# Small vectors loaded as single runs, z's turn in two PSUM places, and a new written order for the opening of a gated scan with two MLPs

## The chip, the cores and the metric

The kernel runs on one core of a Trainium2 chip. The metric is device time in microseconds. The engines are TensorE (PE, with its weight loads as PEld), VectorE (DVE), ScalarE (ACT), GpSimd (POOL) and SyncE (SP, which here only issues DMAs).

## The reference, cut to what matters

```python
# x, f_logit: (1, 6080, 256); lower_bound: (256,)
sig = 1.0 / (1.0 + np.exp(-f_logit))
f = lower_bound + (1.0 - lower_bound) * sig
for t in range(S):
    h = f[:, t] * h + (1.0 - f[:, t]) * x[:, t]
    y[:, t] = h
# first MLP: w_in (256, 2048), w_out (2048, 256), a (4), b (2)
h = y @ w_in
P = a[0] + a[1] * h + a[2] * h**2 + a[3] * h**3
Q = 1.0 + np.abs(b[0]) * np.abs(h) + np.abs(b[1]) * h**2
z = (P / (Q + 1e-6)) @ w_out
# second MLP: its own w_in (256, 2048), w_out (2048, 256)
out = np.maximum(z @ w_in, 0.0) ** 2 @ w_out
```

`f_logit` is called z in the kernel. All weights arrive as 64-bit floats.

## The kernel before

The 6080 tokens are cut into twelve blocks, the first of 448 tokens and the others of 512. Channels lie on the partitions (256 channels are two halves, `dc` 0 and 1), tokens run along the row. The first MLP's 2048 hidden channels are worked off in eight chunks of 256. For block j and chunk i, `mm1` makes h in PSUM (L398 for the very first, L357 for all others), a chain of steps on ScalarE, VectorE and GpSimd makes the ratio P / Q, and `mm2` (L376) adds its product with `w_out` into `acc`. The second MLP does the same with `hb` (L357), `relu` and `r2` (the square) on ScalarE, and `s2` (L376).

From block 2 on a regular loop does this (`S1_mm1`, `S2_mm1` and the rest). Blocks 0 and 1, the conversion of the weights, and block 0's second MLP are the opening. Its order is a list of some 400 steps in the string `FIRST`, written out by hand; each engine takes its own steps in the order of that list. A step's number is its chunk: `0` to `7` are block 0's, `8` to `9` and `A` to `F` block 1's. The second digit, where there is one, is a half. The steps that the prediction speaks of:

- `low`, `scale`, `bits` and a unit such as `i13b` (first MLP's `w_in`, fourth quarter, second half; `o` is `w_out`, `i2`/`o2` the second MLP's): from the 64-bit words, GpSimd (VectorE for i13b, i10b and o10) takes the low bits (L173), ScalarE scales the high ones (L169), VectorE joins them (`bits`, L184).
- `dhi`, `neg`, `dlo`: split a converted weight into a high and a low part for blocks 1 and later: two DMAs issued by GpSimd (L205, L207), and a step on ScalarE (L206) between them.
- `mul00`, `scan00`, `mul01`, `scan01`: block 0's product and scan for the two channel halves, on VectorE (L274, L324). `gate`, `pg`, `mul`, `scan` and `turn`, `in` are the same for block 1, where `gate` needs another table on ScalarE.
- in the chain of a chunk: `abs` or `absq` and `lin` on ScalarE; `sq` on ScalarE (block 0) or on GpSimd (block 1, L756); `poly` on VectorE, two instructions that read h in PSUM (L485, L486); `q` on TensorE (L790) or VectorE; `rsq`, `usq` on ScalarE; `rt` (L809), `rs` (L815), `g` (L520) on VectorE.
- `x1h`, `x1l` and `xbh`, `xbl`: split the scanned block 1 or 2 into a high and a low part (`xbl` on VectorE, L894).

h has one PSUM buffer `h1` in `ps_h` (block 0's odd chunks, and chunk 9, use `acc2` in `ps_a`), so a chunk's `mm1` can begin when the `poly` of the chunk that last had the buffer is done. The loop's first `mm1` follows that of chunk F in `h1`.

Ahead of the list stand the loads: z and x of block 0 as rows of 1 KB on SyncE's queue, three small vectors on ScalarE's (L628 to L630), then the weights, each load 512 KB. TensorE turns z and x (L246) with matmuls on random work around them (`warm`, L653, the fillers).

Of the kernel before, what the change touches and what calls it, by code (L numbers as in the profile page):

```python
# [8 lines left out]
F32 = mybir.dt.float32  # L9
# [5 lines left out]
ALU = mybir.AluOpType  # L15

P = 128
# [9 lines left out]
def hgru_two_moe_kernel(  # L27
# [39 lines left out]
    lbt = const.tile([P, KD], F32, name="lbt")  # L67
# [167 lines left out]
    def first_turn(nm, pool, tag):  # L235
# [3 lines left out]
        if tag == "hb":  # L239
            os = [pool.tile([P, NMAX], F32, tag=tag, name=nm + "t") for _ in range(KD)]  # L240
        else:
            o = pool.tile([P, KD, NMAX], F32, tag=tag, name=nm + "t")
            os = [o[:, dc, :] for dc in range(KD)]
# [381 lines left out]
    with tc.manual_schedule():  # L625
        row_load("z", zf, 0, "A")
        row_load("x", xf, 0, "x2l")
        nc.scalar.dma_start(out=lbt, in_=lower_bound.rearrange("(p k) -> p k", k=KD))  # L628
        nc.scalar.dma_start(out=pna, in_=moe_a.partition_broadcast(P))
        nc.scalar.dma_start(out=pb, in_=moe_b.partition_broadcast(P))  # L630
# [15 lines left out]
        nc.vector.tensor_scalar(out=al, in0=lbt, scalar1=-0.5, scalar2=0.5, op0=ALU.mult, op1=ALU.add)  # L646
        nc.vector.tensor_scalar(out=be, in0=lbt, scalar1=0.5, scalar2=0.5, op0=ALU.mult, op1=ALU.add)
# [9 lines left out]
        warm(diag[:M, 0, :], diag[:M, 0, :], 9)  # L657
        zt = first_turn("z", ps_a, "acc2")
        raw = pt["x", 0]
        warm(diag[:M, 0, :], diag[:M, 0, :], 4)  # L660
        xt = first_turn("x", ps_b, "hb")
        warm(raw[:M, 0, :P], raw[:M, 0, :], 3)
        first_gate(zt)
        nc.scalar.activation(out=pb, in_=pb, func=ACTF.Abs)
# [175 lines left out]
        def other_step(what, arg):  # L840
# [250 lines left out]
```

## Time and profile before

| | us |
|---|---|
| median of 3 runs | 1092.63 (1092.56 to 1092.89) |
| profiled execution, its own time | 1093.02 |
| its span, first to last instruction | 1091.0 |
| TensorE busy | 1076.8 (99%) |
| VectorE busy | 953.9 (87%) |
| ScalarE busy | 878.9 (81%) |
| GpSimd busy | 319.4 (29%) |

Busy times are of the span; a matmul's end is modelled, so a busy TensorE is not one at its peak. The granted clock of TensorE is 1.00 of full speed in nearly all of the span (mean 0.999).

### The profile page before, as it was taken

What the parts mean: (1) busy time and instruction counts of PE and PEld (TensorE: products, weight loads), DVE (VectorE), ACT (ScalarE), POOL (GpSimd) and SP (SyncE); (2) the same over time, 40 slices, a digit from 0 to 9 for tenths busy, and PEclk for the clock granted to TensorE, in tenths of its full rate; (3) what the DMA queues carried; (4) which work ended last, traced back from release to release, by engine and by line L of the source; (5) the groups of instructions that cost most, each with busy time, mean ns of one, the idle gap of its engine ahead of it and who ended that gap; (6) DMA issues with size and microseconds to landing.
All of it is one profiled execution on the core that took longest, in us unless ns stands there. A gap on an engine that the chain in (4) does not pass through costs nothing.

```text
span 1091.0 us, 12474 instructions
## 1 busy us (share of the span) xinstructions
PE 1076.8 (99%) x4596; PEld 859.5 (79%) x4596; DVE 953.9 (87%) x870; ACT 878.9 (81%) x987; POOL 319.4 (29%) x245
## 2 busy tenths in 40 slices
PE   8999999999999999999999999999999999999998
PEld 5457757888888888888888888888888888888887
DVE  6999999899899989989989989989989998998732
ACT  6998767978878888888798887887888878877763
POOL 4875531322312232222231222131222122222100
PEclk9999999999999999999999999999999999999999
DMA  9969512500300300200200120030030020010010
GB/s 325 361 186 211 107 40 54 109 10 1 58 1 1 59 1 1 38 20 1 39 20 1 18 40 1 1 59 1 1 59 1 1 40 19 1 20 1 1 20 20
DMA packets 106444, 53.04 MB, mean 49 GB/s; under 512 B 91920, under 2 KB 93840, under 8 KB 106384
## 3 DMA queue, kind: packets, MB, share of 16 engines
q1 hardware_dynamic: 99968, 35.21, 13.5%
q0 software_dynamic: 4896, 16.78, 6.6%
q8 instruction: 36, 0.59, 0.2%
q10 hardware_dynamic: 1520, 0.27, 0.1%
q14 instruction: 24, 0.20, 0.1%
HBM read 29.23 MB, written 6.23 MB: 33 GB/s over the span
## 4 chain that ended last, share of the span: by engine, by line
PE 89%; DVE 6%; DMA 3%; issue 1%; SPq 1%; DVEq 0%
PE acc L376 45%; PE hb L357 23%; PE h L357 21%; DMA wi<-in_moe_w_in_dram 3%; DVE g L520 1%; DVE s L815 1%; DVE t L809 1%; DVE s L485 1%; DVE s L486 1%; DVE sg L324 1%; DVE t L782 1%; DMA wo<-in_moe_w_out_dram 1%; SPq L130 0%; SPq L232 0%; DVE t L827 0%
## 5 line engine op out<-in xcount | busy, mean ns | idle before, releaser
L357 PE MATMUL hb<-x2h,wi 128*128 128x512 f32 (+1 forms) x768 | 204.4, 388 | 0.0
L577 POOL TENSOR_TENSOR g2l<-r,g2h 128x1024 fp32r<-128x1024 f32 x78 | 188.5, 2416 | 18.3 <-PE acc L376 16.2
L1007 POOL COPY turn<-t 128x1 f32<-128x1 f32 x78 | 14.3, 184 | 559.0 <-DVE t L493 559.0
L357 PEld LDWEIGHTS hb<-x2h,wi 128*128 128x128 f32 x768 | 144.2, 188 | 29.5 <-issue 0.4
L376 PE MATMUL acc<-g2h,wo 128*128 128x512 f32 x664 | 164.2, 389 | 0.0
L376 PEld LDWEIGHTS acc<-g2h,wo 128*128 128x128 f32 x664 | 124.8, 188 | 25.9
L512 ACT ACTIVATE u<-t 128x1024 f32<-128x1024 f32 x80 | 85.0, 1063 | 70.2 <-DVE t L493 70.1
L469 ACT ACTIVATE u<-h,pb 128x1024 f32<-128x1024 f32 x80 | 89.3, 1116 | 60.6 <-PE h L357 60.6
L493 DVE SCALAR_TENSOR_TENSOR t<-t,pb,u 128x1024 f32<-128x1024 f32 x80 | 101.8, 1272 | 30.0 <-ACT t L470 30.0
L486 DVE SCALAR_TENSOR_TENSOR s<-s,pna,h 128x1024 f32<-128x1024 f32 (+1 forms) x96 | 121.9, 1270 | 3.4
L357 PE MATMUL hb<-x2l,wi 128*128 128x512 f32 (+1 forms) x384 | 117.4, 387 | 0.0
L485 DVE TENSOR_TENSOR s<-s,h 128x1024 f32<-128x1024 f32 (+1 forms) x96 | 115.5, 1203 | 1.2 <-ACT s L762 0.8
L539 DVE SCALAR_TENSOR_TENSOR g1h<-s,pna,u 128x1024 fp32r<-128x1024 f32 x80 | 102.4, 1280 | 13.2 <-ACT u L513 7.5
L357 PE MATMUL h<-x1h,wc 128*128 128x512 f32 x352 | 110.3, 394 | 0.9 <-DVE s L486 0.9
L555 ACT ACTIVATE r<-hb 128x512 f32<-128x512 f32 (+1 forms) x178 | 95.5, 586 | 17.7 <-PE hb L357 17.7
L357 PE MATMUL h<-x1l,wc 128*128 128x512 f32 x352 | 108.6, 389 | 0.0
L357 PE MATMUL h<-x1h,wd 128*128 128x512 f32 x352 | 108.5, 389 | 0.0
L542 DVE SCALAR_TENSOR_TENSOR t<-t,g1h 128x1024 f32<-128x1024 f32 x80 | 98.1, 1226 | 9.1 <-DVE g1h L539 0.5
L545 DVE SCALAR_TENSOR_TENSOR t<-s,pna,t 128x1024 f32<-128x1024 f32 x80 | 102.8, 1285 | 2.8
L548 DVE TENSOR_TENSOR g1l<-t,u 128x1024 fp32r<-128x1024 f32 x80 | 98.0, 1225 | 7.7
L561 ACT ACTIVATE r<-r 128x1024 f32<-128x1024 f32 (+1 forms) x95 | 100.0, 1053 | 2.6
L572 ACT ACTIVATE g2h<-r 128x1024 fp32r<-128x1024 f32 x83 | 88.2, 1062 | 14.6 <-PE acc L376 9.3
(153 smaller groups left out, 1895.5 us busy)
## 6 DMA issues: line engine op xcount, KB each, us to landing
wi<-in_moe_w_in_dram SPq DMA_DIRECT2D x16, 512.0 KB, 11.3
wo<-in_moe_w_out_dram SPq DMA_DIRECT2D x16, 512.0 KB, 10.6
out_dram<-o SPq DMA_DIRECT2D x84, 64.0 KB, 2.0
z<-in_f_logit_dram SPq DMA_DIRECT2D x40, 128.0 KB, 3.3
x<-in_x_dram SPq DMA_DIRECT2D x40, 128.0 KB, 3.2
wi<-wa POOLq DMA_DIRECT2D x8, 512.0 KB, 6.5
wo<-whole POOLq DMA_DIRECT2D x8, 512.0 KB, 4.5
wc<-wa POOLq DMA_DIRECT2D x4, 512.0 KB, 6.7
```

Source lines behind the costliest of these rows:

```text
L357: nc.tensor.matmul(out=o, lhsT=ws[a][:, k, fs], rhs=xs[b][:, k, :n], start=(q == 0 and k == 0), stop=(q == len(terms) - 1 and k == KD - 1),)
L376: nc.tensor.matmul(out=acc[dc][:, ts], lhsT=ws[a][:, c, dc::KD] if spread else ws[a][:, c, dc * P:(dc + 1) * P], rhs=gs[b][:, c, ts], star ...
L485: nc.vector.tensor_tensor(out=s, in0=s, in1=h, op=ALU.mult)
L486: nc.vector.scalar_tensor_tensor(out=s, in0=s, scalar=pna[:, 1:2], in1=h, op0=ALU.add, op1=ALU.mult)
L493: nc.vector.scalar_tensor_tensor(out=t, in0=t, scalar=pb[:, 1:2], in1=u, op0=ALU.mult, op1=ALU.add)
L539: nc.vector.scalar_tensor_tensor(out=fh, in0=s, scalar=pna[:, 0:1], in1=u, op0=ALU.add, op1=ALU.mult)
L542: nc.vector.scalar_tensor_tensor(out=t, in0=t, scalar=QC, in1=f32(fh), op0=ALU.add, op1=ALU.mult)
L545: nc.vector.scalar_tensor_tensor(out=t, in0=s, scalar=pna[:, 0:1], in1=t, op0=ALU.add, op1=ALU.subtract)
L548: nc.vector.tensor_tensor(out=fl, in0=t, in1=u, op=ALU.mult)
L555: nc.scalar.activation(out=r[:, c, :], in_=h2.pop((*b, c))[:, :m], func=ACTF.Relu)
L561: nc.scalar.activation(out=r, in_=r, func=ACTF.Square)
L577: eng.tensor_tensor(out=gl, in0=r, in1=f32(gh), op=ALU.subtract)
```

## The change

Three things are changed. The small vectors (`lower_bound`, `moe_a`, `moe_b`) are loaded as one run each into a single partition of a tile `few`, and matmuls with one row of `few` put them on all partitions, in a corner of the PSUM tile `idle`; ScalarE and VectorE read them there. Nine fillers stay ahead of z's turn, the four between z's and x's turn go, and the three behind become four. z's two halves are turned into two PSUM tiles, `acc2` and `acc1`, instead of the two halves of one. And the string `FIRST` holds the same 404 steps in another order.

```diff
-            o = pool.tile([P, KD, NMAX], F32, tag=tag, name=nm + "t")
-            os = [o[:, dc, :] for dc in range(KD)]
+            os = [pool.tile([P, KD, NMAX], F32, tag=g, name=nm + "t")[:, 0, :] for g in (tag, "acc1")]
...
-        nc.scalar.dma_start(out=lbt, in_=lower_bound.rearrange("(p k) -> p k", k=KD))
-        nc.scalar.dma_start(out=pna, in_=moe_a.partition_broadcast(P))
-        nc.scalar.dma_start(out=pb, in_=moe_b.partition_broadcast(P))
+        few = io.tile([P, KD, NMAX], F32, tag="x1l", name="few")
+        nc.scalar.dma_start(out=few[0:1, 0, :D], in_=lower_bound.rearrange("(o f) -> o f", o=1))
+        nc.scalar.dma_start(out=few[0:1, 1, 0:4], in_=moe_a.rearrange("(o f) -> o f", o=1))
+        nc.scalar.dma_start(out=few[0:1, 1, 4:6], in_=moe_b.rearrange("(o f) -> o f", o=1))
+        ones = few[0:1, 1, P:2 * P]
+        nc.vector.memset(ones, 1.0)
...
         warm(diag[:M, 0, :], diag[:M, 0, :], 9)
+        lbt = idle[:, 1, 256:256 + KD]
+        for k in range(KD):
+            nc.tensor.matmul(
+                out=idle[:, 1, 256 + k:257 + k], lhsT=few[0:1, 0, k:D:KD], rhs=few[0:1, 1, P:P + 1], start=True, stop=True
+            )
+        nc.vector.tensor_scalar(out=al, in0=lbt, scalar1=-0.5, scalar2=0.5, op0=ALU.mult, op1=ALU.add)
+        nc.vector.tensor_scalar(out=be, in0=lbt, scalar1=0.5, scalar2=0.5, op0=ALU.mult, op1=ALU.add)
         zt = first_turn("z", ps_a, "acc2")
         raw = pt["x", 0]
-        warm(diag[:M, 0, :], diag[:M, 0, :], 4)
         xt = first_turn("x", ps_b, "hb")
-        warm(raw[:M, 0, :P], raw[:M, 0, :], 3)
+        nc.tensor.matmul(out=idle[:, 1, 256:262], lhsT=ones, rhs=few[0:1, 1, 0:6], start=True, stop=True)
+        warm(raw[:M, 0, :P], raw[:M, 0, :], 4)
         first_gate(zt)
-        nc.scalar.activation(out=pb, in_=pb, func=ACTF.Abs)
+        nc.scalar.activation(out=pb, in_=idle[:, 1, 260:262], func=ACTF.Abs)
+        nc.scalar.activation(out=pna, in_=idle[:, 1, 256:260], func=ACTF.Copy)
...
-            "scale i13b, diag, mul00, scan00, low i13b, scale i10a, scale i10b, bits i13b, mul01, scan01, low "
+            "low i10a, low i13b, scale i10a, mul00, scan00, scale i13b, bits i13b, scale i10b, mm1 0a, mul01, "
```

What the new list does on two engines shows in three places. On VectorE, from block 0's gate (`sg`) to the first `poly` (`s<-s,h`), there stood before (`wa<-wi` alone is `low`, with `wi` and `wa` it is `bits`):

```order
L265 TENSOR_SCALAR sg<-sg,al,be 128x448 x2
L274 SCALAR_TENSOR_TENSOR bx<-sg,xt 128x448
L324 SCALAR_TENSOR_TENSOR x_182<-sg,bx 128x448
L173 TENSOR_SCALAR wa_184<-wi_99 128x512
L184 SCALAR_TENSOR_TENSOR wa_184<-wi_99,wa_184 128x512
L274 SCALAR_TENSOR_TENSOR bx<-sg,xt 128x448
L324 SCALAR_TENSOR_TENSOR x_182<-sg,bx 128x448
L173 TENSOR_SCALAR wa_192<-wi_101 128x512
L184 SCALAR_TENSOR_TENSOR wa_192<-wi_101,wa_192 128x512 x2
L173 TENSOR_SCALAR wb_209<-wo_107 128x1024
L334 COPY carry<-x_182 128x1 x2
L485 TENSOR_TENSOR s<-s,h_200 128x2x448
```

and now:

```order
L263 TENSOR_SCALAR sg<-sg,al,be 128x448 x2
L172 TENSOR_SCALAR wa_183<-wi_100 128x512
L272 SCALAR_TENSOR_TENSOR bx<-sg,xt 128x448
L322 SCALAR_TENSOR_TENSOR x_188<-sg,bx 128x448
L183 SCALAR_TENSOR_TENSOR wa_183<-wi_100,wa_183 128x512
L272 SCALAR_TENSOR_TENSOR bx<-sg,xt 128x448
L322 SCALAR_TENSOR_TENSOR x_188<-sg,bx 128x448
L332 COPY carry<-x_188 128x1 x2
L183 SCALAR_TENSOR_TENSOR wa_181<-wi_102,wa_181 128x512
L172 TENSOR_SCALAR wa_181<-wi_102 128x512
L183 SCALAR_TENSOR_TENSOR wa_181<-wi_102,wa_181 128x512
L172 TENSOR_SCALAR wb_226<-wo_108 128x1024
```

The `low` of i13b has moved ahead of the first product and scan, and the carry copies ahead of the conversions of i10.

On ScalarE, from the gate to the first table load behind it, there stood before (`wi_99` is i13, `wi_101` i10):

```order
L264 ACTIVATE sg<-zt 128x448 x2
L664 ACTIVATE pb<-pb 128x2
L169 ACTIVATE wi_99<-wi_99 128x512
L169 ACTIVATE wi_101<-wi_101 128x512 x2
L855 ACT_TABLE_LOAD
```

and now (`wi_100` is i13, `wi_102` i10):

```order
L262 ACTIVATE sg<-zt 128x448 x2
L670 ACTIVATE pb<-idle 128x2
L671 ACTIVATE pna<-idle 128x4
L168 ACTIVATE wi_102<-wi_102 128x512
L168 ACTIVATE wi_100<-wi_100 128x512
L168 ACTIVATE wi_102<-wi_102 128x512
L862 ACT_TABLE_LOAD
```

One half of i10 is now scaled ahead of i13, and `pna` is copied from PSUM.

On VectorE around `poly F` (here `s<-s,h_1036`, two rows), the last step that reads chunk F's h, there stood before (`x1l<-sg,x1h` are `xbl0` and `xbl1`):

```order
L815 SCALAR_TENSOR_TENSOR s<-s,pna,u 128x1024
L520 SCALAR_TENSOR_TENSOR g<-t,s 128x1024
L782 TENSOR_TENSOR t<-t,u 128x1024
L485 TENSOR_TENSOR s<-s,h_1036 128x1024
L486 SCALAR_TENSOR_TENSOR s<-s,pna,h_1036 128x1024
L894 TENSOR_TENSOR x1l<-sg,x1h 128x512 x2
L809 SCALAR_TENSOR_TENSOR t<-t,u 128x1024
L815 SCALAR_TENSOR_TENSOR s<-s,pna,u 128x1024
```

and now (`poly F` is `s<-s,h_1047`):

```order
L518 SCALAR_TENSOR_TENSOR g<-t,s 128x1024
L901 TENSOR_TENSOR x1l<-sg,x1h 128x512
L822 SCALAR_TENSOR_TENSOR s<-s,pna,u 128x1024
L901 TENSOR_TENSOR x1l<-sg,x1h 128x512
L816 SCALAR_TENSOR_TENSOR t<-t,u 128x1024
L518 SCALAR_TENSOR_TENSOR g<-t,s 128x1024
L789 TENSOR_TENSOR t<-t,u 128x1024
L483 TENSOR_TENSOR s<-s,h_1047 128x1024
L484 SCALAR_TENSOR_TENSOR s<-s,pna,h_1047 128x1024
```

The two low parts of block 2's input have moved from behind `poly F` to ahead of it, between steps of chunks D and E.

## Rows read from the trace of the kernel before

**Rows 1.** The page, busy time of each engine (share of the span).

```profile
PE 1076.8 (99%) x4596; PEld 859.5 (79%) x4596; DVE 953.9 (87%) x870; ACT 878.9 (81%) x987; POOL 319.4 (29%) x245
```

**Rows 2.** Busy time by stretch: stretch, its length, then each engine's busy us.

```profile
core 0: us, PE busy (x) PEld busy (x) DVE busy (x) ACT busy (x) POOL busy (x), PEclk, DMA share, GB/s
8.85:20.00 11.15, 7.79 (x26) 4.04 (x26) 8.87 (x14) 7.78 (x12) 6.32 (x4) 1.00 1.05 386
20.00:60.00 40.00, 37.48 (x106) 18.64 (x105) 39.18 (x44) 39.08 (x54) 32.40 (x15) 1.00 1.06 365
60.00:159.30 99.30, 96.86 (x349) 64.68 (x348) 97.53 (x90) 77.44 (x92) 54.75 (x39) 1.00 0.58 129
...
260.00:1060.00 800.00, 800.00 (x3530) 662.43 (x3529) 709.54 (x632) 653.88 (x717) 199.41 (x158) 1.00 0.10 18
```

**Rows 3.** What TensorE waited for from 0 to 260 us, the largest group.

```profile
PE h L357 <- DVE s L486: 2.9, 3, 1.3
```

**Rows 4.** Order of time on TensorE: start, us, line, idle before it.

```profile
5.35 1.70 PE L246 MATMUL zt<-diag,z 112*128 112x112 f32 x8
...
12.27 3.33 PE L398 MATMUL h<-x,wa 128*128 128x448 f32 x8 [1.68 <-DVE wa L184]
...
159.50 0.70 PE L357 MATMUL h<-x1h,wc 128*128 128x512 f32 x2 [0.88 <-DVE s L486]
```

**Rows 5.** Busy time by stretch, early loads: the last two columns are the DMA's.

```profile
3.00:4.00 1.00, 1.00 (x6) 1.00 (x6) 0.00 (x0) 0.72 (x2) 0.00 (x0) 1.00 0.93 307
4.00:7.00 3.00, 3.00 (x17) 3.00 (x16) 0.24 (x2) 0.00 (x0) 0.00 (x0) 1.00 0.80 218
8.00:9.00 1.00, 1.00 (x11) 1.00 (x10) 0.77 (x3) 0.27 (x3) 0.53 (x1) 1.00 1.04 395
```

**Rows 6.** Order of time on VectorE, the front and the first chain.

```profile
7.67 0.95 DVE L265 TENSOR_SCALAR sg<-sg,al,be 128x448 f32<-128x448 f32 x2 [3.19 <-ACT sg L264]
8.85 0.62 DVE L274 SCALAR_TENSOR_TENSOR bx<-sg,xt 128x448 f32<-128x448 f32 x1 [0.23 <-PE xt L246]
...
10.51 0.81 DVE L173 TENSOR_SCALAR wa<-wi 128x512 int32<-128x512 uint32 x1
11.43 0.69 DVE L184 SCALAR_TENSOR_TENSOR wa<-wi,wa 128x512 int32<-128x512 int32 x1
...
13.70 0.40 DVE L173 TENSOR_SCALAR wa<-wi 128x512 int32<-128x512 uint32 x1
...
17.18 1.11 DVE L173 TENSOR_SCALAR wb<-wo 128x1024 int32<-128x1024 uint32 x1 [1.69 <-DMA wo<-in_moe_w_out_dram]
...
18.69 1.09 DVE L485 TENSOR_TENSOR s<-s,h 128x896 f32<-128x896 f32 x1 [0.28 <-ACT s L762]
...
21.94 1.14 DVE L815 SCALAR_TENSOR_TENSOR s<-s,pna,u 128x896 f32<-128x896 f32 x1
```

**Rows 7.** Order of time on ScalarE: i13b and the first half of i10.

```profile
8.99 0.68 ACT L169 ACTIVATE wi<-wi 128x512 f32<-128x512 f32 x1 [0.71 <-DMA wi<-in_moe_w_in_dram]
...
10.34 0.66 ACT L169 ACTIVATE wi<-wi 128x512 f32<-128x512 f32 x1 [0.67 <-DMA wi<-in_moe_w_in_dram]
```

**Rows 8.** Order of time on VectorE, the end of the opening.

```profile
143.07 1.22 DVE L782 TENSOR_TENSOR t<-t,u 128x1024 f32<-128x1024 f32 x1
...
154.79 2.11 DVE L782 TENSOR_TENSOR t<-t,u 128x1024 f32<-128x1024 f32 x1
...
159.26 1.29 DVE L894 TENSOR_TENSOR x1l<-sg,x1h 128x512 fp32r<-128x512 f32 x2
```

**Rows 9.** Order of time on GpSimd, three of its instructions.

```profile
20.41 3.72 POOL L173 TENSOR_SCALAR wb<-wo 128x1024 int32<-128x1024 uint32 x1
...
65.19 0.92 POOL L207 DMA_DIRECT2D wd<-wa  x1 [2.90 <-ACT wd L206]
...
154.73 3.68 POOL L173 TENSOR_SCALAR whole<-wo 128x1024 int32<-128x1024 uint32 x1
```

**Rows 10.** DMA issues from 0 to 60 us: count, KB each, median us to landing.

```profile
wd<-wa POOLq DMA_DIRECT2D x2, 512.0 KB, 8.4
```

More of the change, by code (lines that the diff above doesn't have):

```diff
@@ L66, in hgru_two_moe_kernel @@
     pb = const.tile([P, 2], F32, name="pb")
-    lbt = const.tile([P, KD], F32, name="lbt")
     al = const.tile([P, KD], F32, name="al")
@@ L645, in hgru_two_moe_kernel @@
         nc.scalar.activation(out=turn, in_=turn, func=ACTF.Tanh)
-        nc.vector.tensor_scalar(out=al, in0=lbt, scalar1=-0.5, scalar2=0.5, op0=ALU.mult, op1=ALU.add)
-        nc.vector.tensor_scalar(out=be, in0=lbt, scalar1=0.5, scalar2=0.5, op0=ALU.mult, op1=ALU.add)
         idle = ps_h.tile([P, 2, NMAX], F32, tag="h1", name="idle")
```

63 rows, old and new, of the table FIRST are left out of this document.

## The prediction

> **What bounds the kernel now.** I read the page's busy times first, then busy time by stretch, then what TensorE waits for, then the order of time on each engine. TensorE is busy 99% of the span and VectorE 87% [rows 1]. From 260 to 1060 us TensorE's 800.00 us are all busy [rows 2]: the steady loop can't give anything, since the change leaves it alone. What can move is the moment at which that loop begins. Its first matmul starts at 159.50, after a wait of 0.88 us for VectorE's L486 [rows 4]: it reuses the PSUM tile of step `mm1 F`, and `poly F`, which ends there, is the last to read it. The loop therefore starts when VectorE has reached `poly F`. Between 20 and 159.3 us VectorE is busy 39.18 of 40.00 and 97.53 of 99.30 us, against TensorE's 37.48 and 96.86 [rows 2], and among TensorE's waits in the opening the largest is for VectorE's `s` [rows 3]. So the opening is limited by VectorE, although TensorE is busier over the whole span.
>
> This makes the account short. Up to `poly F` VectorE does the same steps before and after, with one exception below. The loop's start moves by what changes in four things: when VectorE's stream begins, how long it waits in it, how much its instructions are stretched, and which steps stand ahead of `poly F`.
>
> **Small loads.** The three broadcast loads are 128 rows of 8 or 16 bytes each. While they are in flight the DMA engines move 218 GB/s (4 to 7 us), and afterwards 395 [rows 5]. If 4 to 7 us ran at 390, 3 x 172 = 516 KB more would have moved, or 1.3 us at that rate; the queue of weights behind would land that much earlier. The lower bound is nothing, if the low rate is that of z's and x's 1 KB rows; the nearest row, the 307 GB/s that such rows reached a moment earlier (3 to 4 us, [rows 5]), speaks for a gain, so I take 1.3. The new memset and the copy of `pna` cost VectorE and ScalarE under 0.2 us each in gaps. The three small matmuls have no row. Their bounds are nothing and the price of z's turn, 1.70 us for 8 rows of the trace [rows 4], so 0.2 a row; if the two ahead of z's turn make two rows each, as the fillers do, that is 0 to 0.8, and I take 0.3, since one column is far less than 112.
>
> **Front, step by step.** The nine fillers stay, so z's turn starts at 5.35 + 0.3 = 5.65 and takes 1.70 [rows 4]: its end moves from 7.05 to 7.35. VectorE's two `sg` steps took 0.95 from 7.67 [rows 6] and so ended 1.57 after that. The halves are now apart, so that the first is through by then and one step of about 0.5 is left out of the 1.57: they end at about 7.35 + 1.1 = 8.45. Until then x has landed and been turned, since four fillers are gone between the two. VectorE goes on with `low i13b`, moved here from behind `scan00`: 0.40 us without company (it took 0.81 at 10.51 against 0.40 of its like at 13.70, [rows 6]), to 8.85; then `mul00` and `scan00`, 1.7 us by their starts, to 10.6. ScalarE now scales i10a before i13b. i10a landed at 10.3 and i13b at 9.0 [rows 7]; 1.3 us earlier, ScalarE scales i10a from 9.0 and i13b from 9.7 to 10.3. So `bits i13b` (0.69, [rows 6]) runs from 10.6 to 11.3, and the first real matmul starts at 11.4 instead of 12.27 [rows 4]. The same 0.85 us carries through `scan01`, the first `sq` and `lin` to `poly 0` (before 18.69, [rows 6]), because o10, for which VectorE waited 1.69 us, lands by 15.9 and `low o10` ends by 17.0, ahead of 17.85. **First term: -0.85.** If the small loads change nothing, ScalarE waits for i10a until 10.3, `bits i13b` ends at 12.4, later than before, and the term is +0.2.
>
> **Waits after that.** VectorE waited 0.82 us from 20 to 60 and 1.77 to 159.3 [rows 2]. Adding up the steps in the new order from 14.85 (ScalarE is full: 39.08 of 40, [rows 2]), I find two new ones: `lin 3` now stands behind both gates and a table load and ends at 39.5, where VectorE is there at 38.5; and `usq 5` stands behind `neg i12` and `neg i13`, and VectorE waits 0.65 for it. Some 0.8 of the old waits have no counterpart. Of the new 1.65 about 1.3 fall together with the stretching below: a late VectorE doesn't wait. **Second term: +1.65 - 0.8 - 1.3 = -0.45**, between -0.9 and +0.9.
>
> **Stretched instructions.** Twelve VectorE instructions up to `poly F` take 0.16 to 0.93 us longer than others of their form, 8.3 us in all; the first is `low i13b` (0.81) and the last L782 at 154.79, 2.11 against 1.22 at 143.07 [rows 6, 8]. Each begins within about 1.3 us of a GpSimd instruction's start (here 154.73, [rows 9]), and all but the first take both inputs from SBUF; those that read PSUM, as `poly` does, run at their usual length. GpSimd's list keeps the same eight `sq`, the lows and the gates; only the neighbours change. Which pairs meet can't be read from an order to a fraction of a microsecond. Going through it I find about as many: `bits i13a`, two of the `g`, six of eight `sq`, three lows. **Third term: 0**, the one hit in the first term aside, between -4 and +3.
>
> The Trainium skill's page "SBUF — State Buffer", section "Who interferes with whom", says that a VectorE instruction with two SBUF inputs and a GpSimd instruction that reads SBUF exclude each other, and that the later one waits for the whole of the first. The trace agrees for the short ones and not for the long ones: L815 at 21.94, both inputs in SBUF, begins 1.5 us into a GpSimd `low` of 3.72 us and takes 1.14 [rows 6, 9]. By the page it would have waited until 24.13, 2.2 us; four such meetings in the new order would add some 9 us, to 1101. I go by the row, which gives that no chance.
>
> **Ahead of `poly F`.** The new order puts `xbl0` and `xbl1` before it, which stood behind it and took 1.3 us from 159.26, 1.2 up to the next instruction [rows 8]; they cost the loop's start that much. Before, they were hidden behind the first four of its matmuls. Nothing else changes sides (`q D` and `bits o21` move, but not across it). **Fourth term: +1.2.**
>
> TensorE's own order costs nothing as long as VectorE decides: from 8.85 to 159.3 it has 3.4 + 2.5 + 2.4 us of idle time [rows 2] as cover.
>
> **Sum:** -0.85 - 0.45 + 0 + 1.2 = -0.1 us. The profiled execution took 1093.02 with a span of 1091.0; the runs' median is 1092.63, which is 0.4 below it. The span should stay near 1090.9 and the median near 1092.5.
>
> **Rivals.** *Fewer meetings* (0.25): if the new neighbours halve the stretching, the loop starts about 3.5 to 4 us earlier: 1088.9. For it: six of the twelve lie after 120 us, as the one at 154.79 [rows 8], where a shift by one step would do. Against it: nothing in the order keeps GpSimd's `sq` off them. Its floor is TensorE's own work: 159.50 - 12.27 less 6.8 us idle is 140.4; from 11.4, with some 3 us of waits for ScalarE that stay, the loop begins at 154.8, which is 4.7 us earlier (1087.9).
>
> *More meetings* (0.11): the same at 11 to 12 us of stretching: about 3 us later, 1095.5. It decides from four more hits of 0.9.
>
> *GpSimd late* (0.08, the other side by one mechanism): `mm1 8` now goes before `mm1 9` and needs the low half of i13. Its copy, issued at 65.19 before, when ScalarE had just delivered [rows 9], now queues behind four lows of 3.7 us or more (20.41, [rows 9]), the first of which can't begin before the copies of i10 have landed, by my sum at about 44. That gives an issue at 60.5 and, with the 8.4 us that such copies need [rows 10] a landing at 69; `mm1 8` wants it at 70, and `poly 8` has 2 to 3 us in hand. From four lows of 4.5 instead of 3.7 on it decides, one for one; at 2.5 us the time is 1095.1.
>
> *The small loads don't matter* (0.06): +0.2 instead of -0.85, so 1093.6, still no change by measure.
>
> **How the numbers follow.** About 0.2% (2.2 us) is what a measurement of this kernel can tell from no change. My forecast has 0.50; with the last rival "within 0.2%" has 0.56, faster 0.25, slower 0.11 + 0.08 = 0.19. The range reaches down to the fewer meetings (1089.0) and up to the more (1095.6), and leaves under 2 in 10 outside; the forecast's own range, by its second term and half the third, is 1090.5 to 1094.6.
>
> **What would show it.** Right, if the first matmul after the fillers starts near 11.4, the DMA engines pass 350 GB/s from 4 us on, TensorE's wait before the loop's first matmul is again for `poly F` at about 159, and the stretched instructions again sum to some 8 us. The front is wrong if 12.27 hardly moves; the second term, if VectorE's idle time from 20 to 159 is far from 2.5 us; the third, if stretching is under 5 or over 11 us. The forecast as a whole is wrong if TensorE's opening has no longer VectorE as the engine that it waits for at the end.

## The result, and the profile after

| | before | after |
|---|---|---|
| time, median (lowest to highest) | 1092.83 us (1092.56 to 1093.08, 6 runs) | 1099.44 us (1097.66 to 1104.59, 6 runs) |
| profiled execution, its span | 1093.02, 1091.0 us | 1101.31, 1099.3 us |
| first real matmul / loop's first matmul | 12.27 / 159.50 us [rows 4] | 14.31 / 167.87 us |

The ratio is 1.0066 (95% interval 1.0044 to 1.0088): slower, outside the predicted range. The profiled execution of after is one of its longer ones, 1.9 us above its median; what follows accounts for that execution. The page's busy times and the loop hardly differ from [rows 1, 2]:

```profile
PE 1080.3 (98%) x4596; PEld 861.5 (78%) x4596; DVE 957.3 (87%) x871; ACT 878.9 (80%) x988; POOL 321.6 (29%) x245
```

Busy time by stretch, after (columns as in [rows 2]); the last row is the loop, where TensorE is busy throughout, as before.

```profile
20.00:60.00 40.00, 36.88 (x104) 18.35 (x103) 38.78 (x41) 37.82 (x50) 34.27 (x16) 1.00 0.98 334
95.00:110.00 15.00, 12.97 (x40) 8.40 (x41) 12.03 (x10) 12.08 (x14) 8.76 (x8) 0.89 0.70 167
260.00:1060.00 800.00, 800.00 (x3531) 662.44 (x3530) 713.37 (x636) 654.84 (x719) 201.88 (x160) 1.00 0.10 18
```

So the loss lies ahead of the loop: the span grew by 8.3 us, the loop's start by 8.37. To split it, I take one stretch from the first real matmul to the loop's first, before and then after:

```profile
12.27:159.50 147.23, 140.39 (x469) 86.13 (x469) 142.51 (x142) 122.58 (x153) 91.35 (x55) 1.00 0.73 206
```

```profile
14.31:167.87 153.56, 142.45 (x469) 87.15 (x469) 146.68 (x144) 123.23 (x153) 87.57 (x52) 0.99 0.64 187
```

Read for TensorE: 2.04 us are lost ahead of the stretch, its idle time in it grows from 6.84 to 11.11 (+4.27), and the same 469 matmuls take 2.06 us longer. Read for VectorE: 2.04 ahead, idle 4.72 to 6.88 (+2.16), busy +4.17, of which 1.2 is `xbl0` and `xbl1`, now inside, and most of the rest is stretching: by the count used for the prediction, 14 instructions and 11.0 us against 12 and 8.3 (one of the twelve, 0.41 us, lies ahead of the stretch). Both accounts give 8.37.

**The front.** Order of time on TensorE, then ScalarE, then VectorE:

```profile
5.49 1.01 PE L659 MATMUL idle<-few 1*128 1x1 f32 x4
6.43 1.76 PE L244 MATMUL zt<-diag,z 112*128 112x112 f32 x8
7.99 1.70 PE L244 MATMUL xt<-diag,x 112*128 112x112 f32 x8
...
10.09 1.99 PE L652 MATMUL idle<-x 112*128 112x256 f32 x8
14.31 1.74 PE L396 MATMUL h<-x,wa 128*128 128x448 f32 x4 [2.23 <-DVE wa L183]
```

```profile
12.12 0.17 ACT L670 ACTIVATE pb<-idle 128x2 f32<-128x2 f32 x1 [3.35 <-PE idle L652]
12.19 0.17 ACT L671 ACTIVATE pna<-idle 128x4 f32<-128x4 f32 x1
12.24 1.76 ACT L168 ACTIVATE wi<-wi 128x512 f32<-128x512 f32 x3
```

```profile
13.47 0.69 DVE L183 SCALAR_TENSOR_TENSOR wa<-wi,wa 128x512 int32<-128x512 int32 x1 [2.16 <-ACT wi L168]
```

`pb` and `pna` are read at 12.12 and 12.19. ScalarE waits 3.35 us ahead of them, until the last raw filler (a filler that works on x as it was loaded) is through on TensorE at 12.08: the fillers write other columns of the same PSUM tile `idle` that `pb` is read from, and they stand ahead of the read in program order. All three `scale` steps queue behind that read, `bits i13b` behind them, and the first real matmul behind that.

**The middle.** TensorE again, up to the second MLP's first two `s2` and `mm2 8`, and GpSimd ahead of it:

```profile
97.67 0.67 PE L355 MATMUL hb<-x2h,wi 128*128 128x448 f32 x2 [2.02 <-DMA wi<-wa]
...
98.58 1.56 PE L355 MATMUL hb<-x2h,wi 128*128 128x448 f32 x4
...
100.69 6.90 PE L374 MATMUL acc<-r,whole 128*128 128x448 f32 x16
107.08 2.36 PE L374 MATMUL acc<-g1h,wa 128*128 128x512 f32 x8
```

```profile
85.83 0.58 POOL L204 DMA_DIRECT2D wa<-wb  x1 [3.24 <-DMA wi<-wa]
86.41 0.92 POOL L206 DMA_DIRECT2D wd<-wa  x1
87.41 4.43 POOL L172 TENSOR_SCALAR wa<-wi 128x1024 int32<-128x1024 uint32 x1
91.90 0.58 POOL L204 DMA_DIRECT2D wi<-wa  x1
92.47 0.91 POOL L206 DMA_DIRECT2D wi<-wa  x1
```

`hb 20` is the first to need i21 in its high and low part. Its copies (`dhi`, `dlo`) are issued at 91.90 and 92.47, behind `low i23`. In the kernel before they went out some 12 to 14 us earlier:

```profile
77.58 1.20 POOL L205 DMA_DIRECT2D wi<-wa  x1
...
80.05 0.87 POOL L207 DMA_DIRECT2D wi<-wa  x1
```

TensorE waits 2.02 us, and then the granted clock falls. Busy time by stretch there, first before (95 to 110 us), then after; the third column from the right is the clock:

```profile
95.00:110.00 15.00, 15.00 (x62) 11.39 (x61) 14.50 (x13) 14.09 (x18) 5.58 (x8) 1.00 0.91 206
```

```profile
98.00:99.00 1.00, 1.00 (x6) 0.91 (x5) 0.96 (x2) 0.77 (x1) 1.00 (x2) 0.87 0.00 0
99.00:100.00 1.00, 1.00 (x5) 0.87 (x4) 1.00 (x1) 0.00 (x0) 1.00 (x2) 0.50 1.02 197
...
102.00:103.00 1.00, 1.00 (x4) 0.46 (x3) 1.00 (x1) 1.00 (x2) 0.00 (x0) 0.93 1.01 197
```

From 98.7 to 102.1 TensorE runs at 1.2 instead of 2.4 GHz, half of its clock. That costs 1.7 us, an estimate: half of 3.4 us. The two `s2` (the matmuls `acc<-r,whole`) stand ahead of `mm2 8`, so that VectorE's next step waits in turn:

```profile
109.55 1.29 DVE L830 SCALAR_TENSOR_TENSOR g1h<-s,pna,u 128x1024 fp32r<-128x1024 f32 x1 [2.87 <-PE acc L374]
```

**The end of the opening.** TensorE, VectorE, GpSimd:

```profile
164.20 3.70 PE L374 MATMUL acc<-g,wb3x 128*128 128x512 f32 x8 [1.03 <-DVE g L518]
167.87 0.70 PE L355 MATMUL h<-x1h,wc 128*128 128x512 f32 x2
```

```profile
157.24 1.23 DVE L518 SCALAR_TENSOR_TENSOR g<-t,s 128x1024 f32<-128x1024 f32 x1
...
162.04 2.10 DVE L518 SCALAR_TENSOR_TENSOR g<-t,s 128x1024 f32<-128x1024 f32 x1
```

```profile
160.78 2.29 POOL L763 TENSOR_SCALAR t<-u,pb 128x1024 f32<-128x1024 f32 x1 [12.14 <-ACT u L751]
```

No wait is listed ahead of the loop's first matmul any more, because the matmul before it, `mm2 E`, is late too: it waited for a `g` stretched from 1.23 to 2.10 us by a GpSimd square. But `poly F` still sets the moment. Its second instruction, before and after:

```profile
158.07 1.28 DVE L486 SCALAR_TENSOR_TENSOR s<-s,pna,h 128x1024 f32<-128x1024 f32 x1
```

```profile
166.44 1.28 DVE L484 SCALAR_TENSOR_TENSOR s<-s,pna,h 128x1024 f32<-128x1024 f32 x1
```

It ends at 159.35 and at 167.72, and the loop's first matmul starts 0.15 us behind it both times, at 159.50 and 167.87. The same 0.14 or 0.15 us stand in all but four of the 20 profiles; the four have `sq A` to `sq F` on ScalarE (below).

### The profile page after: what moved, and what is told of

Its sections match the earlier page's. It is cut to its first block, busy times and chain, and to the rows that moved or that the text cites. A ratio compares the mean times of both kernels' runs of the same rounds, so it can differ in the third digit from the quotient of the medians.

```text
span 1099.3 us, 12478 instructions
## 1 busy us (share of the span) xinstructions
PE 1080.3 (98%) x4596; PEld 861.5 (78%) x4596; DVE 957.3 (87%) x871; ACT 878.9 (80%) x988; POOL 321.6 (29%) x245
## 4 chain that ended last, share of the span: by engine, by line
PE 89%; DVE 5%; issue 2%; DMA 2%; ACT 1%; POOL 1%; SPq 0%; POOLq 0%; DVEq 0%
PE acc L374 45%; PE hb L355 23%; PE h L355 21%; DMA wi<-wa 1%; DMA wo<-in_moe_w_out_dram 1%; DVE s L483 1%; PE idle L652 1%; DVE s L822 1%; DVE wb L183 0%; DVE g L518 0%; DVE t L816 0%; DVE sg L322 0%; DVE wa L183 0%; ACT q L757 0%; ACT wi L168 0%
```

## The experiments

Each is timed beside the kernel before on the same chip (medians 1092.84 to 1093.05 us). "Old list" and "new list" are the two orders in `FIRST`, "new front" the new loads and turns. Ratios are to the kernel before.

**Front or list.** The first theory had two causes, ScalarE's wait in the front and i21 in the list; the rival was the front alone. Reading the vectors ahead of the raw fillers:

```diff
-        warm(raw[:M, 0, :P], raw[:M, 0, :], 4)
         first_gate(zt)
         nc.scalar.activation(out=pb, in_=idle[:, 1, 260:262], func=ACTF.Abs)
         nc.scalar.activation(out=pna, in_=idle[:, 1, 256:260], func=ACTF.Copy)
+        warm(raw[:M, 0, :P], raw[:M, 0, :], 4)
```

> The changed kernel with pb and pna read from PSUM ahead of the fillers behind x's turn instead of behind them. Theory 'two causes': ScalarE's 3.35 us wait for the fillers goes, the first real matmul starts near 12.2 instead of 14.31, and the 2 us carry to the end: 1097.4, still slower than before by the list's share; the wait for i21's low part stays. Rival 'front alone': the list was fitted to its own front and only fails because the front is late, so everything comes back: 1093 or less. Rival 'meetings': the front's 2 us are eaten again, 1099.

Measured: 1098.01 us (1095.06 to 1099.24), 1.0043 [1.0028, 1.0058]. The first real matmul came at 12.62. The wait is real, and by the medians it is worth some 1.4 us, with runs that overlap; most of the loss is elsewhere.

The list alone, with the front of before (the string `FIRST` of after in the kernel before), and its counterpart (the string of before in the kernel after):

> The kernel before with the new list alone (old loads, old front). 'Two causes': slower than before by the list's share, 3 to 5 us, with TensorE waiting some 2 us for i21's low part before chunk hb 20 and the granted clock falling to 0.5 for some 3 us behind it: 1096 to 1098. 'Front alone': the list is harmless, 1092 to 1093.5.

Measured: 1100.20 us (1099.79 to 1101.71), 1.0069 [1.0054, 1.0084], more than either theory had. In its profile TensorE waited 1.19 and 2.04 us for i21, and the clock stood at 0.50 from 94.0 to 100.8 us.

> The changed kernel with the old list (new loads, new front, new list undone). 'Two causes': only the front's loss stays, 1.5 to 2.5 us: 1094.5 to 1095.5, no wait for i21's low part. 'Front alone': the whole loss stays, 1098 or more.

Measured: 1093.26 us (1091.87 to 1097.94), 1.0011 [0.9998, 1.0024]. The list carries nearly the whole loss, the front little; that the front alone does it is refuted.

**Which step of the list.** First `low i23` behind the copies of i21, in the kernel after:

```diff
-low i23, x, scale i23, dhi i21, abs 9, scale i22, x2h, neg i21, mm1 A, dlo i21,
+x, scale i23, dhi i21, abs 9, scale i22, x2h, neg i21, mm1 A, dlo i21, low i23,
```

> The changed kernel with one step moved: GpSimd's low i23 (4.4 us) from ahead of dhi i21 and dlo i21 to behind them, so that both copies are issued some 4 us earlier. 'Two causes': TensorE's 2.02 us wait for the copy goes, and with it the 3.4 us at half clock (1.7 us) and VectorE's 2.9 us wait for mm2 8: 1095 to 1097, and the runs spread less. 'Meetings': VectorE's stretched instructions decide anyway, 1099.

Measured: 1099.90 us (1096.75 to 1104.67), 1.0078 [1.0049, 1.0106]. What TensorE waits for from 88 to 112 us:

```profile
PE acc L374 <- DMA wa<-wb: 1.9, 1, 1.9
PE hb L355 <- DMA wi<-wa: 0.3, 1, 0.3
```

Measured against after (1099.44) nothing is gained. The wait for i21 went and came back one step on: `low i23` and `low i22` now stand together ahead of the copies of o10, for which `mm2 8` waits.

So `low i23` was moved forward instead, to GpSimd's idle time (with the vectors read first):

```diff
-poly 6, abs 71, mm2 5, scale o13, x1l0p, neg i20,
+poly 6, abs 71, mm2 5, scale o13, x1l0p, low i23, neg i20,
```

> The new list with the vectors read first (1098.0 us), and low i23 on GpSimd moved ahead from 85 us to just behind x1l0p, where GpSimd idles for 5 us. Theory 'GpSimd's order': the copies of i21 are issued some 4 us earlier, the wait of hb 20 (1.6 us in the profile, 2.0 us and a fall of the clock in others) goes, nothing waits in its place since all later low parts come earlier too, and the time falls by 2 to 4 us to 1094 to 1096 us. Rival 'the loss is spread': another wait takes its place, as when low i23 was moved behind the copies, and the time stays at 1097 to 1099 us.

Measured: 1099.12 us (1097.97 to 1099.78), 1.0055 [1.0041, 1.0069]. No gain: the copies of i21 were issued at 86.7 and 87.7 but queued behind those of o10 and i12, and `hb 20` still waited 1.79 us. That this one `low` step in the wrong place makes the loss is refuted.

Then the list in halves, cut at `mm1 7` (about 62 us), with the vectors read first:

> The old list of steps, the new loads and turns, and the two small vectors read by ScalarE ahead of the raw fillers. With the old list and the vectors behind the fillers the first real matmul came at 13.74 us and the time was 1093.26 us. If that wait of ScalarE is all that the front loses, the first real matmul comes at 12.3 us or before and the time falls by 1.4 us to about 1091.9 us, 1 us under the kernel before. If the front's new parts cost something by themselves (two small matmuls, the turns of z), it stays at 1092.8 to 1093.3 us.

Measured: 1093.76 us (1091.72 to 1096.56, 11 runs), 1.0010 [0.9999, 1.0020]. Its first real matmul came at 11.22 in the profile, 2.5 us ahead of the same list with the vectors behind the fillers (13.75), but the median is no lower (1093.26 there): the gain that was expected did not come.

> New loads and turns, vectors read first, the old list up to mm1 7 (about 62 us) and the new order of the steps behind it. Theory 'GpSimd's order': low i23 stands late as in the new list, so most of the loss stays, 1096 to 1098 us. Rival 'the loss is spread': about half of the 6 us goes, 1094 to 1095 us. If the loss sits in the first half, 1091 to 1093 us.

Measured: 1095.72 us (1095.56 to 1099.44), 1.0034 [1.0021, 1.0047].

> The counterpart: the new list up to mm1 7 and the old order of the steps behind it. Theory 'GpSimd's order': low i23 stands early again, as in the old list; 1092 to 1093.5 us. Rival 'the loss is spread': 1094 to 1096 us. If the loss sits in the first half, 1096 to 1098 us.

Measured: 1096.29 us (1094.89 to 1097.33), 1.0029 [1.0018, 1.0040]. Against 1093.76 us the halves cost 2.0 and 2.5 us, together about what the whole new list costs with the same front (1098.01 - 1093.76 = 4.3): the loss is spread, as the rival had it, though the runs of each group lie 2 to 5 us apart, so the split is rough.

All five steps of i21 earlier (and `z`, a load of block 2, behind them), with the front of before. The lines are shortened, and the five old places, from which the steps go, are left out:

```diff
-dlo i20, usq 6, z, poly 7, scale o20, q 71, rsq 71, ... usq 7, scale o21, scale i21, g 6,
+dlo i20, usq 6, scale i21, poly 7, scale o20, q 71, bits i21, dhi i21, rsq 71, ... usq 7, neg i21, dlo i21, z, scale o21, g 6,
```

> The kernel before with the new list (1100.2 us), and the five steps of i21 (scale, bits, neg, dhi, dlo) moved ahead by some 10 us, to where GpSimd and its DMA queue idle, z behind them. Theory 'i21 late': the 2 to 3 us of waits for hb and the fall of the granted clock behind them (0.81 over 15 us, 2.9 us) go: 1095.5 to 1097 us, clock 1.00 throughout. Rival 'the loss is spread': what waits is something else next, 1099 to 1100 us.

Measured: 1096.90 us (1096.80 to 1098.16), 1.0036 [1.0023, 1.0049], against 1100.20 with the list alone. What TensorE waits for from 12 to 168 us, the first line:

```profile
PE acc L376 <- DVE g L520: 3.7, 3, 1.5
```

The wait for i21's copies is gone, and with it the fall of the clock behind it, and the wait of VectorE for `mm2 8` (4.1 us with the list alone): 3.3 of 7.4 us. What is left is VectorE, for whose `g` TensorE now waits 3.7 us.

**Ahead of `poly F`.** Moving `xbl1` and `xbl0` back behind it, alone and with i21 early:

```diff
-g D, xbh1, xbl1, mm1 F, usq E, xbh0, rs E, lin F, xbl0, abs F, ... s2 5, poly F, usq F,
+g D, xbh1, mm1 F, usq E, xbh0, rs E, lin F, abs F, ... s2 5, poly F, xbl1, xbl0, usq F,
```

> The kernel before with the new list (1100.2 us, 1099.8 to 1101.7), and xbl1 and xbl0 moved back behind poly F. The prediction's fourth term said that they cost 1.2 us where the new list has them: then 1099 us. In the trace of the new list the last mm2 waits 1.0 us for g E, behind which nothing is late, and xbl1 and xbl0 stand ahead of g E on VectorE: taken away from there g E comes earlier, but the loop's first matmul then waits for xbl as in the kernel before (0.9 us): 1100 us, no change.

Measured: 1098.37 us (1096.03 to 1100.88, 4 runs), 1.0051 [1.0035, 1.0067].

> As the one with i21 early, and xbl1 and xbl0 behind poly F as in the kernel before. Moved alone they gave 1098.4 instead of 1100.2 us, with a scatter of 5 us. If the two parts add up: 1094 to 1095.5 us. If the move of xbl is worth nothing, 1095.5 to 1097 us.

Measured: 1097.08 us (1096.04 to 1097.93), 1.0037 [1.0023, 1.0051]. Alone 1.8 us by the medians, with i21 early nothing; the runs of either lie 2 to 5 us apart. What the two steps cost is not settled beyond "0 to 2 us". Of the four runs with `xbl` behind alone, the two faster (1096.03 and 1097.02) have a mean granted clock of 1.000 and 0.999, the two slower (1099.72 and 1100.88) 0.998 and 0.997; the list alone had 0.997 or 0.998 in all four. So the 1.8 us may be the clock's. And as `hb 20` waits 2.03 us in the profile of 1097.02 too, without a fall of the clock, much of the 3.3 us that i21 gave back may be the fall's and not the wait's; no run separates the two.

**The price of stretching.** In the kernel before, `sq A` to `sq F` on ScalarE instead of GpSimd:

```diff
+                elif n >= 10:
+                    nc.scalar.activation(
+                        out=k["t"], in_=k["u"], func=ACTF.Identity, scale=pb[:, 1:2], bias=pb[:, 0:1]
+                    )
```

> The kernel before, with the six steps sq A to sq F on ScalarE instead of GpSimd (same result, Identity with scale and bias). In its profile five of the stretched VectorE instructions, 4.3 us of 8.3, meet these steps. Theory 'meetings count': VectorE sets the pace of the opening, each us of stretching is a us of the end, so the time falls by 2 to 4 us to 1089 to 1091 us; this would also mean that the 1.3 to 5 us of added stretching with the new list are lost time. Rival 'TensorE's waits decide': the stretching is hidden, 1092.5 to 1093 us. A third way: six more instructions on ScalarE (1.2 us each) delay other steps, 1094 us or more.

Measured: 1091.74 us (1091.38 to 1092.26, 11 runs), 0.9989 [0.9981, 0.9998]. The stretching fell from 8.3 to 4.3 us, the loop began at 157.87 (no wait; `poly F` had ended 0.25 us earlier), and the time fell by 1.1 us. Busy time by stretch, up to that matmul:

```profile
12.00:157.87 145.87, 139.68 (x468) 86.18 (x469) 138.60 (x142) 129.34 (x159) 84.04 (x49) 1.00 0.73 209
```

VectorE is busy 3.9 us less than before for the same 142 instructions, but idle 7.3 instead of 4.7 us: of 4 us saved, 2.5 turned into waits. What VectorE waited for from 12 to 157.9 us, the first line:

```profile
DVE t L786 <- ACT t L756: 2.5, 2, 2.1
```

ACT L756 is a square on ScalarE. So the new waits are the edit's own price, and the run does not measure what a us of stretching costs by itself. The same on the new list, with i21 early and `xbl` behind:

> As the one with i21 early and xbl behind, and sq A to sq F on ScalarE. On the kernel before that gave 1.1 us for 4.0 us less stretching. Theory 'meetings count': 1.1 us or more here too, 1092.5 to 1094 us. If the new list's faults are these three, it then stands within 1.5 us of the old list with the same squares (1091.74 us); if it stays 3 us or more behind, the loss is in its other waits.

Measured: 1101.95 us (1100.32 to 1105.12), 1.0085 [1.0071, 1.0099]. The stretching fell there too (to 4.4 us, 6 instructions), and the time rose. What TensorE waits for from 60 to 170 us:

```profile
PE h L357 <- DVE s L486: 3.7, 1, 3.7
PE hb L357 <- ACT r L911: 2.4, 1, 2.4
```

With six more steps on ScalarE a `relu` comes late, and then VectorE's `s`; that less stretching must help is refuted for this order and this way of getting it. Part of the rise is the clock's: it stood at 0.50 from 12.4 to 15.8 and from 152.3 to 155.8 us in the profile, and its mean is 0.995 to 0.997 in all four runs. What delays the `relu` was not followed further.

**The front's scatter.** With the new front, the vectors read first and the old list the same kernel takes 1091.7 in one execution and 1096.6 in another; the kernel before stays within 1 us in every group. Three changes to it: four fillers put back between z's and x's turns (the edit shown); z turned into one tile as before, which leaves the new loads, their small matmuls and the new fillers; then that with the squares on ScalarE:

```diff
         raw = pt["x", 0]
+        warm(diag[:M, 0, :], diag[:M, 0, :], 4)
         xt = first_turn("x", ps_b, "hb")
```

> The old list with the new loads and turns and the vectors read first (1093.76 us, 1091.72 to 1096.56), and the four fillers on diag put back between z's and x's turns. Its profile had the first real matmul at 11.22 us and ended 0.7 us before the kernel before, but other executions were 3 to 4 us longer, most of them with a lower mean clock. Theory 'clock': the missing fillers leave TensorE idle ahead of the first gates, the clock falls in some executions, and with the fillers the scatter goes: 1091.5 to 1092.5 us, highest under 1094 us. Rival 'arrival': the scatter comes from when the loads land; it stays, highest 1096 us or more.

Measured: 1093.55 us (1091.49 to 1096.18, 11 runs), 1.0006 [0.9997, 1.0015]. The scatter stays.

> The old list, the new loads with the vectors read first, and z turned into one tile as before; so the edit of z's halves alone is taken out. If the halves are worth nothing, the time and the scatter are those with both edits, 1091.7 to 1096.6 us, and the first real matmul stays near 11.2 us. If the halves carry the gain of the front, the first real matmul comes 0.3 us later or more; if they carry the scatter, it goes and the time lies within 0.5 us of 1092 us.

Measured: 1093.52 us (1092.30 to 1096.34, 10 runs), 1.0009 [1.0000, 1.0018]. The scatter stays without z's halves. The loads, the small matmuls that go with them and the fillers are left; no run parts the loads from the matmuls.

> The old list, the new loads with the vectors read first, z as before (1093.52 us, 1092.3 to 1096.34), and sq A to sq F on ScalarE. Theory 'scatter by meetings': an earlier front shifts GpSimd against VectorE, and the squares that meet it differ from one execution to the next; without them the scatter goes, 1090.7 to 1091.5 us, highest under 1093 us. Rival 'arrival': the scatter comes from the loads of the front themselves, highest 1095 us or more, median 1091.5 to 1092.5 us.

Measured: 1093.63 us (1091.09 to 1094.98, 11 runs), 1.0003 [0.9994, 1.0012]. The squares are not the cause, but its profile caught an execution of 1094.98 us. Order of time on TensorE in it:

```profile
6.43 1.77 PE L245 MATMUL zt<-diag,z 112*128 112x112 f32 x8
7.99 1.70 PE L245 MATMUL xt<-diag,x 112*128 112x112 f32 x8
...
10.54 3.78 PE L653 MATMUL idle<-x 112*128 112x256 f32 x8 [0.33 <-ACT pna L671]
14.38 3.82 PE L397 MATMUL h<-x,wa 128*128 128x448 f32 x6
```

And in the profile with the vectors read first and the old list (1092.23 us):

```profile
5.91 1.21 PE L244 MATMUL zt<-diag,z 112*128 112x112 f32 x8
6.96 1.12 PE L244 MATMUL xt<-diag,x 112*128 112x112 f32 x8
...
8.72 1.99 PE L652 MATMUL idle<-x 112*128 112x256 f32 x8 [0.33 <-ACT pna L670]
11.22 3.34 PE L396 MATMUL h<-x,wa 128*128 128x448 f32 x8 [0.51 <-DVE wa L183]
```

The same eight matmuls take 1.77 or 1.21 us, the same eight fillers 3.78 or 1.99. TensorE starts at half its rate and reaches the full one at some moment, before z's turn in the second and not before the first real matmul in the first. The profile of after shows a middle case, half rate up to x's turn (1.70) and full in the raw fillers (1.99). Of the eleven profiles with the two small matmuls of `lower_bound` ahead of z's turn six have x's turn at 1.70, of the nine others none (1.10 to 1.22). The count is not clean: seven of the nine have the old front, with four fillers between the two turns. So the two matmuls were moved behind z's turn, first alone, then with the squares on ScalarE:

```diff
         warm(diag[:M, 0, :], diag[:M, 0, :], 9)
+        zt = first_turn("z", ps_a, "acc2")
         lbt = idle[:, 1, 256:256 + KD]
 ...
-        zt = first_turn("z", ps_a, "acc2")
```

> The old list, the new loads and turns, vectors read first (1093.76 us, 1091.72 to 1096.56), and the two small matmuls of the lower bound with their two reads moved behind z's turn. In the traces so far TensorE issues the same small matmuls at 0.21 us at first and 0.12 us from some moment on: 4.7 to 5.3 us in profiles of this front that were fast, 9.7 us or later in those that were slow, 5.2 to 7.3 us in all with the old front. Theory 'late full rate': the small matmuls with their waits ahead of z's turn put that moment off; behind z's turn it comes by 7.5 us in every execution, the first real matmul by 11.8 us, and the time is 1091.5 to 1092.5 us, highest under 1094 us. Rival 'arrival': the scatter stays, highest 1095.5 us or more.

Measured: 1092.54 us (1091.62 to 1094.92, 11 runs), 0.9997 [0.9988, 1.0006]; first real matmul at 11.11. Ten of eleven runs lie at or under 1093.3 us, where with the small matmuls ahead five of eleven did; one is at 1094.9. The scatter is smaller, not gone. Nor does the rate explain all of it: this profile, at the full rate from z's turn on, took 1093.29 us, and its loop began at 159.82, 0.32 us later than before.

> As the one with the lower bound behind z, and sq A to sq F on ScalarE (alone on the kernel before: 1091.74 us, 1091.38 to 1092.26). If both gains add up: 1090.3 to 1091.3 us, under every kernel so far. If the gain of the front is lost behind it: 1091.5 to 1092 us.

Measured: 1091.29 us (1090.57 to 1094.73, 11 runs), 0.9989 [0.9980, 0.9997]. By the median the lowest of all, 1.6 us under the kernel before, with some scatter left; the kernel before with the squares on ScalarE alone (1091.74) is the steadier, and the two can't be told apart by their intervals. Both beat the kernel before and after. The early front has no part in the profiled execution (1091.29 us): z's and x's turns ran at the full rate (1.25 and 1.21 us), and then the granted clock stood at 0.50 from 9.2 to 12.6 us, so that the raw fillers took 3.57 us and the first real matmul came at 12.56.

```profile
8.93 3.57 PE L652 MATMUL idle<-x 112*128 112x256 f32 x8 [0.33 <-ACT pna L670]
```

## Why the prediction was wrong

The frame of the prediction held: `poly F`, the last of VectorE's stream, starts the loop, before and after. Three of its four terms were too low. By VectorE's account of the profiled execution they came to 2.04 + 2.16 + 2.7 + 1.2, 8.1 of 8.37 us. No single step explains it, and the account is that of one execution. With the same list in other runs the loss stands elsewhere (stretching by the same count, up to the loop; the rows of the last two below):

| us | first real matmul | VectorE idle from there to the loop | stretching (instructions) | loop's first matmul |
|---|---|---|---|---|
| before | 12.27 | 4.72 | 8.3 (12) | 159.50 |
| after | 14.31 | 6.88 | 11.0 (14) | 167.87 |
| new list, old front | 13.08 | 8.50 | 8.8 (11) | 166.26 |
| after, vectors read first | 12.62 | 3.51 | 12.5 (15) | 164.47 |

```profile
13.08:166.26 153.18, 143.66 (x469) 88.01 (x469) 144.68 (x144) 123.42 (x153) 90.40 (x54) 0.98 0.66 193
```

```profile
12.62:164.47 151.85, 142.03 (x469) 85.56 (x469) 148.34 (x144) 122.80 (x153) 88.03 (x52) 1.00 0.66 193
```

With the list alone, which carries nearly the whole loss by the experiments, the waits of the second term are the largest part and the stretching hardly grew; with the vectors read first it is the other way round. What the runs share is the list, not the term.

**First term** (-0.85 us; measured +2.04). The working had ScalarE scale i10a from 9.0; it did so from 12.24. What failed is the sentence that the copy of `pna` costs "under 0.2 us in gaps": its length was right (0.17), its place in the queue was not. It and the read of `pb`, which the working does not price, read a tile that the raw fillers write, and stand behind them. With that wait taken away and TensorE early at its full rate, the first real matmul comes at 11.22, 11.18 and 11.11 in three profiles, but these have the old order of steps in the front; the new order with the wait taken away was caught only with a late full rate, at 12.44 to 12.62, and so the predicted 11.4 is neither shown nor refuted. Beside it, the lower bound's two matmuls delayed z's turn by 1.08 us (5.35 to 6.43), not 0.3: their four rows took 1.01 us at half rate (0.63 at the full one), however few columns they have. The size of the small loads was nearly right: the weights came 1.0 us earlier, not 1.3. DMA issues, the load of i13b, issued at 1.69 before and after: count, KB, us to landing:

```profile
wi<-in_moe_w_in_dram SPq DMA_DIRECT2D x1, 512.0 KB, 7.3
```

```profile
wi<-in_moe_w_in_dram SPq DMA_DIRECT2D x1, 512.0 KB, 6.3
```

i10a landed at 9.33 instead of 10.32. The reason given was not quite right: from 4 to 7 us the rate rose from 218 to 280 GB/s, not to 390, and part of the gain came from 2 to 3 us (104 to 245 GB/s).

Nor does what the front loses or gains carry to the end in full, as the working had it. The front alone (old list, first real matmul at 13.75) cost 0.4 us by the medians, and in the run with the lower bound behind z the first real matmul came 1.16 us earlier than before and the loop 0.32 us later.

**Second term** (-0.45; VectorE's idle time measured +2.16, with the list alone +3.78). Of the four terms this is the one whose failure the experiments show: moving i21 forward gave 3.3 us back, the wait and the clock together. Adding up VectorE and ScalarE in the new order missed that VectorE would have to wait for TensorE. The sentence that failed is "TensorE's own order costs nothing as long as VectorE decides": behind `s2 0` and `s2 1`, which now stand ahead of `mm2 8`, VectorE waited 2.87 us at 109.55 (4.1 us with the list alone, nothing with i21 early). The rival *GpSimd late* had the right mechanism, a low half whose copy queues behind `low` steps, and the wrong weight: it watched i13 (issued at 63.01, in time), and it was i21, issued 12 to 14 us later than before. The run with i21 early shows it: 3.3 us come back.

**Third term** (0, between -4 and +3; stretching measured +2.7). *More meetings* named 11 to 12 us, and 11.0 came, or 12.5 with the vectors read first; the list alone has 8.8. So in after the size lies within the range, with the vectors read first it lies above it, and nothing shows what moves it. Its price, a stretched us as a us of the loop's start, no run measures: where 4.0 us were taken away, VectorE waited 2.5 us for the squares in their new place.

The rule of the Trainium skill's page "SBUF — State Buffer", section "Who interferes with whom", that the later one waits for the whole of the first, fits the squares to about 0.2 us: the `g` at 162.04 ended at 164.14, against 163.07, the square's end, plus its own 1.23. It does not fit the lows: a `bits` at 93.88 took 2.14 us within a `low` that ran from 93.47 to 97.53. That the time came near the 1101 us which the prediction worked out from that rule is chance: meetings with lows took up to 1.1 us each, and not the rest of the low.

**Fourth term** (+1.2; 0 to 1.8 by two experiments). In the trace the two steps take 1.2 us of VectorE ahead of `g E` and `poly F`, as the working had it. What they cost in time stays open.

Not settled either: the rest of the list's loss, some 4 us with i21 early. By the halves it is spread over both; with i21 early it shows as waits for VectorE's `g`. Which steps make it was not tried, so more than half of the loss has no cause shown.

## What to carry to other kernels

A read of a few columns waits for everything queued ahead of it that writes the same tile (3.35 us here): put small PSUM reads ahead of fillers, or in a tile of their own, and ask what stands behind the read on its engine. When an order is new, follow each weight from its last conversion step through the copy queue to its first use, on all engines at once; here the place where the chain was late was not the one first suspected, and moving one step only moved the wait. A wait that no view lists can still decide: compare a start with the end of everything that it depends on, as with `poly F`. And taking 4 us of stretching from an engine that is busy 98% of a stretch gave 1.1 us, because the work that was moved away came back late: price the new place of a step as well as the old one.

## What the runs showed of the hardware

- TensorE's rate at the start is a matter of the execution. The column of the granted clock says 1.00 there, but z's eight matmuls take 1.10 to 1.25 us in nine of the 20 profiles and 1.68 to 1.77 in eleven. The Trainium skill's page "TensorE: Matmul & The Clock Gate", section "What's actually happening", says that TensorE is throttled to half rate by default, that activity releases it, and that the moment differs from one execution of the same kernel to the next. The rows agree with the two rates and with the scatter; that matmuls of one column ahead of z's turn put the moment off is what the counts above speak for, not proof of it.
- A wait of 2.0 us was followed by 3.4 us at 0.50 of the clock in after, waits of 1.19 and 2.04 us by 6.8 us at 0.50 with the list alone, and one of 2.03 us by none in the run with `xbl` behind `poly F`, where the clock stayed at 1.00. So a wait's price here is its length or about twice it, and the profiles do not show what decides. In the front the clock fell to 0.50 for some 3.5 us in four of the 20 profiles, two with the old loads (i21 early, from 13.7 us, and that with `xbl` and squares, from 12.4) and two with the new ones (`low i23` behind i21, from 12.7, and the last experiment, from 9.2).
- Copies queue: with `low i23` early i21's were issued at 86.72 and 87.73, 4.7 to 5.2 us earlier than in after, but behind two others of 512 KB issued at 85.57 and 86.15, and `hb 20` began at 95.31, only 2.4 us earlier, of which 1.8 are the front's.
